# Hashed attention and a channel mix on one core: the last output tile in three column pieces, and a new order of all operations

## The chip, the cores and the metric

The kernel runs on one core of a Trainium2 chip. The metric is device time in microseconds, the median of several runs; a profiled execution gives the trace. The core has five engines with their own instruction streams: TensorE (PE; its weight loads are shown as PEld), VectorE (DVE), ScalarE (ACT), GpSimd (POOL) and SyncE (SP), which here issues nearly all DMA transfers. Every stream is executed in its program order, so an instruction that waits holds up all that stand behind it on its engine or queue.

## What is computed

Two stages, one feeding the other. The first is attention over 4 batches, 8 heads, 768 positions and 64 features, in which a query sees only the keys of its own hash bucket; a bucket is the six signs of a projection. The second mixes each position with the one before it and runs a squared-relu layer with a sigmoid gate.

```python
def _attn_ref(q, k, v, proj):
    ...
    q_bits = (np.einsum('bhsd,dk->bhsk', q, proj) > 0).astype(np.int64)
    k_bits = (np.einsum('bhsd,dk->bhsk', k, proj) > 0).astype(np.int64)
    ...
    mask = q_bucket[:, :, :, None] == k_bucket[:, :, None, :]
    scores = scale * np.matmul(q, k.transpose(0, 1, 3, 2))
    scores = np.where(mask, scores, -1000000000.0)
    ...
    return np.matmul(attn, v).astype(np.float32)

def _moe_ref(x, mu_k, mu_r, w_k, w_v, w_r):
    x_prev = np.concatenate([np.zeros((B, 1, D), dtype=np.float32), x[:, :-1, :]], axis=1)
    xk = mu_k * x + (1.0 - mu_k) * x_prev
    xr = mu_r * x + (1.0 - mu_r) * x_prev
    k = np.maximum(xk @ w_k, 0.0)
    v = k * k @ w_v
    r = 1.0 / (1.0 + np.exp(-(xr @ w_r)))
    return (r * v).astype(np.float32)
```

The attention output, heads side by side, is x: 4 x 768 x 512. The weights are 512 x 1024, 1024 x 512 and 512 x 512.

## The kernel before

**Pairs.** The 32 heads are worked on as 16 pairs n = 0 to 15, four to a batch. For each pair, q, k and v are loaded (ldq, ldv; 384 KB each, pair 0 in quarters of 192 KB). Each side is split into a high and a low fp16 part: hi (lines 535 and 537, for pairs 0 and 1 lines 609 and 611) and lo (line 540, or 614). A transposing DMA (tr, line 544) brings it into the layout for TensorE; pairs 0 and 1 use TensorE transposes instead (line 628), with copies out of PSUM (line 632). The bits matmuls (line 568, or 650 for pair 0) give the sign projections; bx (line 572) turns them into rows, and small DMAs (row, line 592) write these into the same tile as q and k, so that the score matmul adds a penalty for differing buckets by itself. Then follow nine score groups of 1024 columns (sc, line 701), each with its exponential on ScalarE (line 705); the PV matmuls (oo, lines 729 and 734), the first of which reads a column sum of v (the casts and sums va and vsum, lines 482, 490, 493, 496); the normalization (rc and ob, lines 744 to 751); and a transpose of the result into xt, by DMA (otd, line 761) or TensorE (ot, line 787), with small shift copies (xs and xj, lines 769 to 774).

**Channel mix.** VectorE forms the mixed inputs (df, xk and xr, lines 822 to 834). Once four pairs of a batch are ready, its first layer runs in 16 groups (kp, line 852), each evicted by a relu on ScalarE or VectorE (lines 857 and 859) and squared on VectorE (sq, line 862). For each of six row tiles there is a gate matmul (r, line 877), a tanh (line 880), the second layer (v, line 889), the gated product on VectorE (os, line 896) and a store (st, line 900). The weights are loaded in ten pieces of 512 KB (wl, line 428) and cast (wc, lines 431 to 433).

**The order.** Each operation is added to a plan with its engine, what it reads and writes, and an estimated cost. Three tables written into the file then decide everything: `WHERE` gives the engine of operations that may run on several, `SLOT` the PSUM bank of each result, and `ORDER` the place of each operation in one list for all engines. The plan walks that list:

```python
        order = [self.ops[i] for i in ORDER]
        for o in order:
            if o.take is not None:
                name, size = o.take[1], BANKS[o.take[0]]
                self.slot[name] = SLOT[name]
```

So the priorities and costs in the file have no effect on the emitted program; the tables have.

**The last tile.** The last row tile of the last batch is made in two column pieces, in one PSUM bank:

```python
            for lo, hi in ((0, DM // 2), (DM // 2, DM)) if last else ((0, DM),):
                ...
                        r=[...] + ([(nv, 0)] if lo and g == 0 else []),
                        w=[(nv, lo)], take=("sm", nv, 1) if g == 0 and lo == 0 else None, name=nv)
```

The second piece's matmuls come after VectorE's read of the first, since the two share the bank.

Of the kernel before, what the change touches and what calls it, by code (L numbers as in the profile page):

```python
# [32 lines left out]
def X(kind, n):  # L33
    return PX.get(f"{kind}@{n}", 0.0)


def R(kind, n):
# [193 lines left out]
def kernel(  # L231
# [17 lines left out]
    DM = H * D  # L249
# [4 lines left out]
    NFC = DF // P  # L254
# [89 lines left out]
    add = plan.add  # L344
# [613 lines left out]
```

## Time and profile before

| | us |
|---|---|
| median of 3 runs | 250.81 (249.42 to 251.02) |
| profiled execution, its own time | 251.54 |
| its span, first to last instruction | 249.8 |
| TensorE busy | 234.7 (94%) |
| VectorE busy | 196.9 (79%) |
| ScalarE busy | 179.2 (72%) |
| GpSimd busy | 28.6 (11%) |

Times are in microseconds from the span's start unless they are marked otherwise. Matmuls are pipelined, and the mean of one in the profile is longer than the distance from one to the next; the lengths in the chain are such distances. A wait is put down to what ended it. "PEclk" is the TensorE clock that was granted; its mean over the span is 0.998 of full speed. The share of the sixteen DMA engines in a stretch can come out a little over 1, because packets overlap.

### The profile page before, as it was taken

The numbers are of one execution on the slowest core, as the hardware profiler recorded it, in microseconds if no ns is written. First come the engines' busy times: TensorE is split into PE (matmuls) and PEld (weight loads), VectorE is DVE, ScalarE is ACT, GpSimd is POOL, SyncE is SP. The second block draws the span as 40 slices with busy tenths as digits, with TensorE's granted clock in tenths as the row PEclk, the third lists the DMA queues.
The fourth block names the chain that finished last, engine by engine and source line by source line (L and its number), as shares of the span: only waits on it lengthen the run. The fifth ranks groups of instructions, "written<-read, shape, count | busy, mean of one in ns | idle before, by whom it ended". The sixth has DMA issues, their size and how long they took to land.

```text
span 249.8 us, 6514 instructions
## 1 busy us (share of the span) xinstructions
PE 234.7 (94%) x2611; PEld 147.1 (59%) x2611; DVE 196.9 (79%) x471; ACT 179.2 (72%) x224; POOL 28.6 (11%) x75
## 2 busy tenths in 40 slices
PE   7685999999969999999999999999999999999993
PEld 3453778877636656565567576664865654555442
DVE  3997499899879898889998898899697878376322
ACT  4695899999969989896779889988787223332220
POOL 5003141422202410100001100100000000000000
PEclk9999999999999999999999999999999999999999
DMA  6998989999899979899998997792231031022223
GB/s 192 314 199 279 219 269 163 307 175 220 281 332 190 307 152 316 218 187 287 188 342 158 159 186 192 194 235 41 90 64 45 0 129 41 1 84 87 84 85 126
DMA packets 74154, 44.56 MB, mean 178 GB/s; under 512 B 54476, under 2 KB 69132, under 8 KB 74124
## 3 DMA queue, kind: packets, MB, share of 16 engines
q1 hardware_dynamic: 74028, 44.15, 71.6%
q8 instruction: 20, 0.33, 0.5%
q14 instruction: 10, 0.08, 0.1%
q10 hardware_dynamic: 96, 0.01, 0.0%
HBM read 24.12 MB, written 6.29 MB: 122 GB/s over the span
## 4 chain that ended last, share of the span: by engine, by line
PE 81%; DVE 8%; DMA 5%; ACT 1%; SPq 1%; issue 1%; DVEq 0%
PE ps_all L701 21%; PE ps_all L889 17%; PE ps_all L852 16%; PE ps_all L734 13%; PE ps_all L877 8%; PE ps_all L568 4%; DMA nat<-in_q_dram 4%; DMA a<-bx 2%; DVE nh L540 1%; DVE nh L614 1%; PE ps_all L729 1%; DVE a L658 1%; ACT pt L705 1%; SPq L592 1%; PE ps_all L787 1%
## 5 line engine op out<-in xcount | busy, mean ns | idle before, releaser
L705 ACT ACTIVATE pt<-ps_all 128x1024 bf16<-128x1024 f32 x144 | 138.9, 1034 | 21.5 <-PE ps_all L701 20.1
L701 PE MATMUL ps_all<-a 128*128 128x512 f16 (+3 forms) x408 | 79.8, 316 | 3.9 <-DMA a<-bx 2.9
L852 PE MATMUL ps_all<-xk,wk 128*128 128x384 bf16 x256 | 49.0, 326 | 2.3 <-DVE kr L859 2.3
L701 PEld LDWEIGHTS <-a 128*128 128x128 f16 x408 | 35.1, 97 | 25.1 <-DMA a<-bx 3.1
L889 PE MATMUL ps_all<-wv,k 128*128 128x512 bf16 (+1 forms) x200 | 45.9, 370 | 0.6 <-DVE os L896 0.6
L734 PEld LDWEIGHTS <-pt 128*128 128x128 bf16 x1152 | 41.3, 97 | 6.6 <-issue 0.4
L734 PE MATMUL ps_all<-va,pt 128*128 128x65 bf16 x1152 | 43.2, 193 | 0.0
L852 PEld LDWEIGHTS <-wk 128*128 128x128 bf16 x256 | 24.4, 98 | 19.1 <-issue 2.9
L889 PEld LDWEIGHTS <-k 128*128 128x128 bf16 x200 | 19.4, 98 | 20.6 <-issue 0.7
L880 ACT ACTIVATE rs<-ps_all 128x512 f32<-128x512 f32 x24 | 14.2, 601 | 21.0 <-PE ps_all L877 19.1
L857 ACT ACTIVATE kr<-ps_all 128x384 bf16<-128x384 f32 x33 | 15.8, 491 | 17.6 <-DVE k L862 11.2
L896 DVE SCALAR_TENSOR_TENSOR os<-rs,ps_all 128x512 f32<-128x512 f32 (+1 forms) x25 | 16.5, 663 | 14.7 <-PE ps_all L889 9.8
L540 DVE SCALAR_TENSOR_TENSOR nh<-nat,nh 128x768 f16<-128x768 f32 x28 | 26.8, 958 | 1.1 <-ACT nh L535 0.6
L862 DVE TENSOR_TENSOR k<-kr 128x384 bf16<-128x384 bf16 x64 | 22.1, 360 | 3.7 <-ACT kr L857 3.5
L859 DVE TENSOR_SCALAR kr<-ps_all 128x384 bf16<-128x384 f32 x31 | 17.1, 555 | 8.8 <-PE ps_all L852 6.5
L877 PE MATMUL ps_all<-wr,xr 128*128 128x512 bf16 x96 | 23.8, 379 | 0.0
L751 DVE TENSOR_TENSOR ob<-ps_all,rc 128x384 bf16<-128x384 f32 (+1 forms) x36 | 18.3, 511 | 1.0
L877 PEld LDWEIGHTS <-xr 128*128 128x128 bf16 x96 | 9.1, 97 | 9.7
L537 DVE TENSOR_SCALAR nh<-nat 128x768 f16<-128x768 f32 x22 | 12.7, 576 | 1.6 <-DMA nat<-in_q_dram 1.6
L568 PE MATMUL ps_all<-a,p0g 128*32 128x256 f16 (+1 forms) x180 | 13.3, 276 | 0.5 <-DVE ob L751 0.2
L568 PE MATMUL ps_all<-a,p1g 128*32 128x256 f16 (+1 forms) x180 | 12.9, 273 | 0.0
L834 DVE TENSOR_TENSOR xk<-tm,xt 128x768 bf16<-128x768 f16 (+1 forms) x18 | 10.0, 558 | 0.2
(95 smaller groups left out, 187.5 us busy)
## 6 DMA issues: line engine op xcount, KB each, us to landing
vn<-in_v_dram SPq DMA_DIRECT2D x16, 384.0 KB
out_dram<-os SPq DMA_DIRECT2D x23, 256.0 KB
nat<-in_k_dram SPq DMA_DIRECT2D x15, 384.0 KB
nat<-in_q_dram SPq DMA_DIRECT2D x15, 384.0 KB
wst<-in_moe_w_k_dram SPq DMA_DIRECT2D x2, 512.0 KB
wst<-in_moe_w_r_dram SPq DMA_DIRECT2D x2, 512.0 KB
wst<-in_moe_w_v_dram SPq DMA_DIRECT2D x2, 512.0 KB
a<-bx SPq DMA_DIRECT2D x48, 9.0 KB
```

What stands on the lines that cost most here:

```text
L540: nc.vector.scalar_tensor_tensor(out=nh[:, :, D:P], in0=nat.rearrange("p j (c d) -> p (j c) d", d=D), scalar=QS, in1=nh[:, :, 0:D], op0=AL ...
L568: nc.tensor.matmul(ps[g_ * wid : (g_ + 1) * wid, 0:FW], w_[:, m_ - 1 - x : m_ - 1 - x + wid], a_t[sa][:, i, x % NFOLD * FW : (x % NFOLD + ...
L701: nc.tensor.matmul(ps[:, lo - s * w : hi - s * w], side_a["k"][sa][:, j, jc * P : (jc + 1) * P], side_a["q"][sa][:, j, q0 : q0 + hi - lo], ...
L705: nc.scalar.activation(out=pt_t[sp][:, s * w : (s + 1) * w], in_=ps_all[:, plan.slot[nm] * 512 : plan.slot[nm] * 512 + w], func=AF.Exp, bi ...
L734: nc.tensor.matmul(oo[:, (ic - c0) * 65 : (ic - c0) * 65 + 65], pt_t[sp][:, o : o + P], va_t[sa][:, j, jc, 0 : D + 1], start=(not uc and i ...
L751: nc.vector.tensor_tensor(out=ob_t[so][:, c0:c1, j * D : (j + 1) * D], in0=oo[:, :, 0:D], in1=rc_t[sr][:, 1, c0:c1].unsqueeze(2).to_broadc ...
L852: nc.tensor.matmul(ps[:, 0:HALF], wk_sb[:, d, fc * P : (fc + 1) * P], xk_t[mx[d]][:, h * HALF : (h + 1) * HALF], start=(d == 0), stop=(d = ...
L859: nc.vector.tensor_scalar(out=kr_t[sk], in0=sm(nm)[:, 0:HALF], scalar1=0.5 ** 0.5, scalar2=0.0, op0=ALU.mult, op1=ALU.max)
L862: nc.vector.tensor_tensor(out=k2_t[s2][:, h * HALF : (h + 1) * HALF], in0=kr_t[sk], in1=kr_t[sk], op=ALU.mult)
L877: nc.tensor.matmul(sm(nr), xr_t[mx[d]][:, c * P : (c + 1) * P], wr_sb[:, d, :], start=(d == 0), stop=(d == NDC - 1))
L889: nc.tensor.matmul(sm(nv)[:, lo:hi], k2_t[(b * NFC + fc) % NK2][:, c * P : (c + 1) * P], wv_sb[:, fc, lo:hi], start=(fc == 0), stop=(fc == ...
L896: nc.vector.scalar_tensor_tensor(out=os_t[so][:, lo:hi], in0=rs_t[s1][:, lo:hi], scalar=1.0, in1=sm(nv)[:, lo:hi], op0=ALU.add, op1=ALU.mult)
```

## The change

Two things are changed. The last tile is made in three column pieces of 256, 128 and 128, each with a PSUM bank of its own, an own read on VectorE and an own store. And the three tables are replaced as a whole: all operations but those of the last tile stay the same, while their order, the banks and the engine of 88 of them differ. There is no other edit; in the changed file the lines stand one to four further down.

```diff
 WHERE = {
-    "wc0": "DVE", "wc1": "POOL", ... "hi0q0": "ACT", "evt0q00": "DVE", ...
+    "wc0": "POOL", "wc1": "POOL", ... "hi0q0": "DVE", "evt0q00": "ACT", ...
 ...
 ORDER = [
-    0, 2, 3, 4, 5, 6, 7, 8, 1, 67, 64, 98, 99, 25, 9, 35, ...
+    65, 67, 0, 2, 3, 4, 40, 25, 41, 5, 92, 1, 10, 93, 94, 6, ...
 ...
+    LASTCUT = (0, 256, 384, 512)
 ...
-            for lo, hi in ((0, DM // 2), (DM // 2, DM)) if last else ((0, DM),):
+            cut = LASTCUT if last else (0, DM)
+            for lo, hi in zip(cut[:-1], cut[1:]):
+                nv = f"v{b}_{c}" if lo == 0 else f"v{b}_{c}_{lo}"
+                ko = ("os", so) if lo == 0 else ("os2", so, lo)
 ...
-                        r=[...] + ([(nv, 0)] if lo and g == 0 else []),
-                        w=[(nv, lo)], take=("sm", nv, 1) if g == 0 and lo == 0 else None, name=nv)
+                        r=[...],
+                        w=[(nv,)], take=("sm", nv, 1) if g == 0 else None, name=nv)
```

On SP's queue the changed order issues the v loads of pairs 0 and 2 ahead of the k and q loads of pair 3, and the loads of pairs 10 and 11 later than before. In each table the position of an operation can be read off; the prediction counts along them.

More of the change, by code (lines that the diff above doesn't have):

```diff
@@ L891, in add_moe @@
                     add("PE", 4 * MM(hi - lo), T + 0.12 + 0.12 * g, fv,
-                        r=[("wv", fc) for fc in range(4 * g, 4 * g + 4)] + [("k2", (b * NFC + fc) % NK2, h) for fc in range(4 * g, 4 * g + 4) for h in (c // 3,)] + ([(nv, 0)] if lo and g == 0 else []),
-                        w=[(nv, lo)], take=("sm", nv, 1) if g == 0 and lo == 0 else None, name=nv)
+                        r=[("wv", fc) for fc in range(4 * g, 4 * g + 4)] + [("k2", (b * NFC + fc) % NK2, h) for fc in range(4 * g, 4 * g + 4) for h in (c // 3,)],
+                        w=[(nv,)], take=("sm", nv, 1) if g == 0 else None, name=nv)
                 def fo(nv=nv, s1=s1, so=so, lo=lo, hi=hi):
@@ L900, in st @@
                     nc.sync.dma_start(out=rows[:, lo:hi], in_=os_t[so][:, lo:hi])
-                add("DVE", DVE_C(hi - lo), T + PR["os"] + X("os", b), fo, r=[(nv, lo), ("rs", s1)] + ([] if lo == 0 else [("os", so)]), w=[("os", so)] if lo == 0 else [("os2", so)],
-                    give=[nv] if hi == DM else [], name=f"os{b}_{c}")
-                add("SP", 0.45, T + PR["os"] + X("os", b), st, r=[("os", so)] if lo == 0 else [("os2", so)], svc=0.65 if hi - lo == DM else 0.33, off=0.85, land=0.7, name=f"st{b}_{c}")
+                add("DVE", DVE_C(hi - lo), T + PR["os"] + X("os", b), fo, r=[(nv,), ("rs", s1)] + ([] if lo == 0 else [("os", so)]), w=[ko], give=[nv], name=f"os{b}_{c}")
+                add("SP", 0.45, T + PR["os"] + X("os", b), st, r=[ko], svc=0.65 * (hi - lo) / DM + 0.03 * (hi - lo < DM), off=0.85, land=0.7, name=f"st{b}_{c}")
     for n in range(NPAIRS):
```

228 rows, old and new, of tables (ORDER, SLOT, WHERE) are left out of this document.

## The prediction

> **What bounds the kernel now.** I read the page first: busy time, the slices, the DMA rows and the chain.
>
> ```profile
> span 249.8 us, 6514 instructions
> PE 234.7 (94%) x2611; PEld 147.1 (59%) x2611; DVE 196.9 (79%) x471; ACT 179.2 (72%) x224; POOL 28.6 (11%) x75
> ...
> DMA  6998989999899979899998997792231031022223
> ...
> q1 hardware_dynamic: 74028, 44.15, 71.6%
> ...
> HBM read 24.12 MB, written 6.29 MB: 122 GB/s over the span
> ...
> PE 81%; DVE 8%; DMA 5%; ACT 1%; SPq 1%; issue 1%; DVEq 0%
> ```
>
> TensorE is busy for all but 15.1 us, and its work is the same in both kernels, so the change can only move that idle time and the tail. But the DMA engines are full too, from the start until slice 27 (27 x 6.2 = 169 us). Two limits run side by side: TensorE's own work, and the transfers that must have landed before its next work may start. The waits and the stretches (columns after the times: PE, PEld, DVE, ACT, POOL busy, clock, DMA share, GB/s) say where TensorE's idle time lies.
>
> ```profile
> PE ps_all L701 <- DMA a<-bx: 2.9, 1, 2.9
> PE ps_all L852 <- DVE kr L859: 2.3, 1, 2.3
> PE ps_all L628 <- DVE nh L614: 1.4, 2, 1.0
> ...
> PE ps_all L889 <- DVE os L896: 0.6, 1, 0.6
> ...
> 8.00:9.00 1.00, 1.00 (x9) 0.63 (x8) 1.00 (x4) 0.99 (x3) 0.00 (x0) 1.00 1.06 361
> ...
> 20.00:30.00 10.00, 7.09 (x100) 5.05 (x99) 5.10 (x10) 6.98 (x8) 2.90 (x6) 1.00 1.00 253
> ...
> 70.00:80.00 10.00, 7.38 (x76) 4.72 (x74) 8.34 (x16) 7.82 (x11) 1.43 (x3) 1.00 1.07 260
> ...
> 170.00:180.00 10.00, 10.00 (x158) 6.74 (x157) 7.91 (x24) 7.68 (x9) 0.00 (x0) 1.00 0.17 60
> 240.00:250.00 10.00, 5.98 (x35) 3.22 (x33) 2.43 (x5) 1.58 (x3) 0.00 (x0) 0.93 0.28 106
> ```
>
> The idle time sits ahead of 30 us, at 70 us and in the tail; from 80 to 240 us TensorE hardly stops. The clock is full. The chain (start, length, what) shows that both large holes are late transfers:
>
> ```profile
> 20.91 4.03 DMA a<-bx
> ...
> 65.69 5.27 DMA nat<-in_q_dram
> ...
> 143.91 0.84 PE ps_all L568 x24
> ```
>
> At 20.91 a small sign-row transfer takes 4.03 us because it queues behind loads. At 65.69 pair 8's q load takes 5.27 us; VectorE stands at hi8 until it lands, and the PSUM evictions behind hi8 are what line 852 waits for (2.3).
>
> **The price of a transfer.** One 384 KB load (393 kB) at 361 GB/s and a share of 1.06 is 1.15 us of all sixteen engines; 512 KB of weights is 1.54, an output tile 0.77, a quarter-pair load 0.58, sign rows nearly nothing. The queue's total is 71.6% of 249.8 = 178.9 us. HBM traffic, 30.41 MB at that rate, is 89.3; the rest, 89.6 us, belongs to 28 transposes of twelve blocks and 11 of six, 33.5 whole ones: an estimate of 2.67 us each (1.33 for a small one).
>
> **The queue test.** For each point where TensorE waits for a transfer I add up the transfers up to and including it on SP's queue, and TensorE's own work ahead of it in program order. The work is counted in the order at the paces of the chain:
>
> ```profile
> 103.25 1.73 PE ps_all L889 x8
> ...
> 115.66 0.87 PE ps_all L701 x5
> ...
> 153.85 0.65 PE ps_all L852 x4
> ...
> 159.49 1.09 PE ps_all L734 x36
> ```
>
> That is 0.216 us for 512 columns, two score groups in 0.87, 0.163 for 384 columns, 0.030 for 65. Transfer sum minus work is the idle time that the order forces, less a lag that is alike for both orders. Check on before: the last transpose of pair 7 has four quarter loads, 20 loads, two weights and twelve transposes up to it, 2.3 + 23.0 + 3.1 + 32.0 = 60.4 us; TensorE reached that pair's bit matmuls (line 568) at 63.66, as the timeline has it (start, length, what, idle time before and what ended it; hi8's row stands below it):
>
> ```profile
> 63.66 0.69 PE L568 MATMUL ps_all<-a,p0g 128*32 128x256 f16 x4 [0.21 <-DVE ob L751]
> ...
> 70.99 0.56 DVE L537 TENSOR_SCALAR nh<-nat 128x768 f16<-128x768 f32 x1 [1.56 <-DMA nat<-in_q_dram]
> ```
>
> So the lag is at most 3.3 us, and 60.4 + 3.3 leaves no slack. Work ahead of it is 50.0, so 10.4 us are forced beside the lag.
>
> **Part one, the order.** In the changed order the same matmuls stand behind 55 score groups instead of 51; 53.0 us of work covers 62.0 us of transfers (one weight more): 9.0 are forced. Pairs 10 to 14 give 11.8, 11.1, 11.6, 12.7, 10.8 before and 8.9, 9.3, 8.0, 9.6, 9.3 after. Idle time once taken stays, so the largest counts: 12.7 before, 9.6 after, a relief of 3.1 us. Pair by pair from 7 to 15 the mean relief is 1.9. Before reached pair 13's bits at 143.91 where its floor is 137.9 + 3.3 = 141.2, so it lost 2.7 more to other things. If the new order loses the same above its own floor, the relief is what comes out. I take 2.5, between 1.9 and 3.1. Ends: nothing (the time comes back as waits on other engines), and 3.1 + 2.7 if those go too.
>
> The opening gives nothing by this test: ahead of pair 1's second row transfer both orders have four quarter loads, ten loads and two transposes, 19.2 us, under the same 14.7 us of work. New there: two v loads are issued earlier and keep the queue fed, so the 4.03 us wait may shrink by up to its 2.9 of idle; but pair 2's rows, now with 22.6 us of transfers under 18.6 of work where it was 21.5 under 20.1, take it back. I put zero, with 0 and 2.9 us of gain as the ends.
>
> At hi8 the new order puts two evictions of line 859 ahead of the waiting hi8 on VectorE. Queued behind it are then lo8 and the later evictions, and meanwhile TensorE has three score groups, the rest of a PV group and two first-layer groups (about 2.8 us) of work that needs none of them. That covers a wait like the 1.56 us of this trace; without the cover the 2.3 us stall returns. What is late next are the loads of pairs 10, 11 and 14, which stand some 10 us deeper in the queue (94.2, 108.5 and 136.8 us of transfers): VectorE or ScalarE would stand there. At 3.3 to 6.3 us of lag (hi8 had the upper one: it began at 70.99 with 64.7 us of transfers) they force idle time only up to 17.1, at pairs 10 and 14, which before had passed by then as well.
>
> **Part two, other engines.** In net numbers eleven first steps of the v sums, six second steps, one third step, two v casts, three weight casts (one of them off VectorE) and two small copies go to GpSimd.
>
> ```profile
> L490 DVE TENSOR_TENSOR vt<-va 128x390 f32<-128x390 bf16 x7 | 3.9, 558 | 0.0
> ...
> L493 DVE TENSOR_TENSOR vt<-vt 128x130 f32<-128x130 f32 x4 | 1.2, 295 | 0.6 <-POOL vt L490 0.5
> ...
> L482 POOL CAST va<-vn 128x768 bf16<-128x768 f32 x6 | 6.0, 1001 | 24.2 <-DMA vn<-in_v_dram 16.9 <-PE ps_all L734 5.3 <-PE ps_all L701 2.0
> L496 POOL TENSOR_TENSOR vsu<-vt 128x130 bf16<-128x130 f32 x5 | 2.4, 477 | 18.5 <-DVE vt L493 16.8 <-PE ps_all L568 1.7
> L493 POOL TENSOR_TENSOR vt<-vt 128x130 f32<-128x130 f32 x4 | 1.7, 436 | 12.0 <-DVE vt L490 12.0
> L431 POOL CAST wk<-wst 128x1024 bf16<-128x1024 f32 x1 | 1.0, 1040 | 0.0
> L490 POOL TENSOR_TENSOR vt<-va 128x390 f32<-128x390 bf16 x1 | 0.8, 837 | 0.0
> ```
>
> VectorE is relieved of 11 x 0.56 + 7 x 0.29 and about 1.8 for casts, 10.0 us; GpSimd gains 11 x 0.84 + 7 x 0.44 + 2 x 1.00 + 3 x 1.04 and about 1 for copies, 18.5 us on 28.6. Its idle time (89%) hides that, so I put it at zero. Without cover it is the third rival. Switched hi, relu and copy operations between ScalarE and VectorE nearly cancel in count: zero.
>
> GpSimd's work could also slow VectorE. The trace has one sign of it, the third figure here (shortest, median, longest, ns):
>
> ```profile
> L537 DVE TENSOR_SCALAR nh<-nat x22: 547/552/1062, 9.6 to 148.4; 128x768 f16<-128x768 f32 x22
> ```
>
> One of 22 took 0.51 us longer than the median. The Trainium skill, "SBUF — State Buffer" (section "SBUF: two separate sides"), says that the two engines share a port pair as an exclusive lock, held for a whole instruction, so that the later one stands still. By that rule at its worst, every added GpSimd microsecond is taken from VectorE; this trace's one long case in 22 is far from that.
>
> **Part three, the last tile.** Now two pieces of 256 columns share one bank, so the second waits for VectorE's read of the first:
>
> ```profile
> 243.04 1.90 PE L889 MATMUL ps_all<-wv,k 128*128 128x512 bf16 x12
> ...
> 245.04 0.42 DVE L896 SCALAR_TENSOR_TENSOR os<-rs,ps_all 128x256 f32<-128x256 f32 x1 [0.24 <-PE ps_all L889]
> 245.51 1.03 PE L889 MATMUL ps_all<-wv,k 128*128 128x256 bf16 x8 [0.57 <-DVE os L896]
> ...
> 246.58 0.42 DVE L896 SCALAR_TENSOR_TENSOR os<-rs,ps_all 128x256 f32<-128x256 f32 x1 [1.12 <-PE ps_all L889]
> ```
>
> ```profile
> L896 DVE SCALAR_TENSOR_TENSOR os<-rs,ps_all 128x512 f32<-128x512 f32 x23 | 15.6, 684 | 13.4 <-PE ps_all L889 8.5 <-ACT rs L880 2.8 <-ACT kr L857 1.1
> ...
> L900 SPq DMA_DIRECT2D out_dram<-os x25: 332/333/819, 114.2 to 247.0; - x25
> ```
>
> The tile begins four 512-column matmuls after 243.04, at 243.90. After: eight matmuls of 256 and sixteen of 128 columns at the same pace per column, 1.75 us, with nothing between; 0.20 from there to VectorE (246.58 less 245.51 less 0.87); a 128-column read, by the slope from 0.68 at 512 columns to 0.42 at 256, 0.29. It ends at 246.14 instead of 247.00: 0.86 us gained.
>
> The extra store issue, 0.33, fits in the 0.44 us between the second and third read; uncovered it would leave 0.53. Eight more matmuls and weight loads are in the pace.
>
> **Sum.** 2.5 + 0.86 = 3.36. The profiled execution took 251.54 us around its span of 249.8, which becomes 248.2; it was 0.73 above the median, so on the median of 250.81 the forecast is 247.5 us.
>
> **Rivals.** First, the order gives back what it gains: TensorE was 94% busy, and VectorE, ScalarE and the queue are all near full before 80 us, so a stall taken from one shows at the next. Then only the tail counts: 250.0. This is also how it comes out if the reorder doesn't do what it says.
>
> Second, all that before lost above its floor goes as well: 250.81 - 0.86 - 3.1 - 2.7 = 244.1. For it speaks that hi8 alone was 2.3; against it, that other waits of this sort were all over the opening.
>
> Third, slower: the v sums on GpSimd. Each tile's PV begins with a matmul that reads the sum, and everything behind it on TensorE waits. A whole chain is 0.84 + 0.44 + 0.48 on GpSimd against 0.56 + 0.29 + 0.29, 0.6 us more, and in order: pair 4's last step now stands behind pair 5's cast, which waits for pair 5's load (52.0 us of transfers). Eleven of these are 6.6 us; with half uncovered, 250.81 - 0.86 + 3.3 = 253.3. A harsher form is VectorE standing still while GpSimd works (the 0.51 us above): at its worst the added 18.5 less the relief of 10.0 is lost, 247.5 + 8.5 = 256.0; I give it 0.03 of the case's 0.20. The chain decides from about 0.3 us of uncovered wait per moved chain on. Against it: the order leaves most of the sums of pairs 7 to 14 several microseconds ahead of their matmul.
>
> **How the numbers follow.** Forecast 0.47, tail only 0.23, all gone 0.10, slower 0.20. A measurement of this kernel tells about 1% from no change (249.42 to 251.02 here), so faster means below 248.3. The forecast's own spread (245 to 249) gives 0.40 faster and 0.07 within; tail only 0.20 within and 0.03 slower; all gone 0.10 faster; the slower case 0.17 slower and 0.03 within. Together 0.50, 0.30, 0.20. The range runs from near the second rival to near the third, 244.5 to 253.0.
>
> **What would show it.** Right: pair 7's bits start near 62.0 + 3.3 = 65.3 with four score groups more behind them; pair 13's by 141.5; no wait of line 852 above 1 us around 70 us; the last tile's matmuls without a stop. Wrong: waits of the PV matmuls for GpSimd sums; VectorE or ScalarE standing at the loads of pairs 10, 11 or 14 with evictions behind; pair 13's bits later than 144.

## The result: slower by 1.0 to 1.5%, and the profile after

The changed kernel took 253.68 us (252.56 to 253.93, four runs) beside 250.92 for the kernel before: ratio 1.015, interval 1.0108 to 1.0192; a second series gave 1.0139 (1.0080 to 1.0197). Ratios, here and below, are of fast runs alone, since some executions fall into a slower state; the medians of all runs give 1.011 and 1.010. The forecast was 247.5. The profiled execution, at 252.56 us the quickest of its four, stands only 1.0 us over the profiled one of before, so the two traces show less than half of the 2.8 us between the medians; more traces follow below. The page:

```profile
span 250.8 us, 6530 instructions
...
PE 236.3 (94%) x2619; PEld 147.8 (59%) x2619; DVE 191.2 (76%) x449; ACT 178.2 (71%) x223; POOL 50.0 (20%) x99
...
PE 74%; DMA 9%; DVE 9%; SPq 4%; issue 2%; ACT 1%; DVEq 0%
```

GpSimd has 21.4 us more (18.5 were worked out), but VectorE only 5.7 less, where 10.0 were worked out. In the chain TensorE fell from 81% to 74%. The stretches of before (first fence) and after (second; PE, PEld, DVE, ACT, POOL busy, clock, DMA share, GB/s):

```profile
18.00:26.00 8.00, 5.09 (x61) 3.48 (x58) 6.05 (x11) 4.59 (x6) 2.14 (x5) 1.00 0.91 274
60.00:90.00 30.00, 27.05 (x343) 17.95 (x342) 25.88 (x62) 26.69 (x34) 6.02 (x10) 1.00 0.97 249
```

```profile
18.00:26.00 8.00, 6.30 (x65) 3.98 (x66) 6.16 (x11) 6.35 (x8) 0.00 (x0) 1.00 0.64 138
60.00:90.00 30.00, 27.22 (x347) 17.93 (x348) 28.65 (x62) 25.61 (x30) 12.64 (x18) 1.00 0.95 250
```

Two things stand out: from 18 to 26 us the transfer queue is a third empty, and from 60 to 90 us VectorE is busy 28.65 of 30 us, beside a GpSimd with twice the work. What TensorE waits for (total, times, longest):

```profile
PE ps_all L702 <- DMA a<-bx: 2.5, 4, 1.0
PE ps_all L702 <- ACT pt L706: 1.8, 4, 0.8
PE ps_all L629 <- DVE nh L615: 1.7, 2, 1.2
...
PE ps_all L853 <- DVE kr L860: 1.1, 2, 0.9
```

No wait for GpSimd is among them. The two large holes of before (2.9 and 2.3) are gone, and many of about half a microsecond took their place. The chain from 66 to 84 us shows why:

```profile
66.91 3.38 DMA a<-bx
70.28 0.54 DVE ob L752
...
73.15 1.01 DVE kr L860 x2
...
74.46 0.95 DVE tm L831
...
76.36 0.77 DVE nh L538
77.13 0.90 DVE k L863
...
80.28 0.78 DVE nh L538
81.09 0.96 DVE nh L541
...
83.38 0.34 PE ps_all L730
```

For 13 us the chain hardly leaves VectorE. And several of its instructions are stretched. The timeline of VectorE and GpSimd in the changed kernel:

```profile
74.46 0.83 POOL L483 CAST va<-vn 128x768 bf16<-128x768 f32 x1 [6.88 <-DMA vn<-in_v_dram]
74.46 0.94 DVE L831 TENSOR_SCALAR tm<-df,mu 128x384 f16<-128x384 bf16 x1
...
75.36 0.85 POOL L491 TENSOR_TENSOR vt<-va 128x390 f32<-128x390 bf16 x1
75.43 1.00 DVE L835 TENSOR_TENSOR xk<-tm,xt 128x384 bf16<-128x384 f16 x1
...
76.66 1.16 POOL L483 CAST va<-vn 128x768 bf16<-128x768 f32 x1
...
77.05 0.97 DVE L863 TENSOR_TENSOR k<-kr 128x384 bf16<-128x384 bf16 x1
...
78.93 0.81 PE L853 MATMUL ps_all<-xk,wk 128*128 128x384 bf16 x4 [0.94 <-DVE kr L860]
```

An operation of 0.35 us (line 863) takes 0.97 when it falls on a GpSimd cast, and ends 0.21 us after that. In the two traces of the changed kernel all four executions of this line that took over 0.3 us too long ended 0.21 to 0.22 us after the GpSimd instruction they met, however long they were. The relu eviction behind it (line 860) is what TensorE then waits for. Executions of three lines, by the tiles they work on (shortest, median, longest, ns):

```profile
L831 DVE TENSOR_SCALAR tm<-df,mu x20: 276/416/1187, 38.3 to 133.2; 128x768 f16<-128x768 bf16 x12, 128x384 f16<-128x384 bf16 x8
L863 DVE TENSOR_TENSOR k<-kr x64: 310/351/973, 77.0 to 241.1; 128x384 bf16<-128x384 bf16 x64
L860 DVE TENSOR_SCALAR kr<-ps_all x29: 508/550/558, 73.1 to 233.2; 128x384 bf16<-128x384 f32 x29
```

Line 860 reads PSUM and is never stretched. I call *excess* the time of VectorE's instructions above the median of their line and shape, where that is over 0.06 us. Before it is 3.5 us in 9 instructions, after 9.8 us in 26, and each of the 35 overlaps a GpSimd instruction, although in the changed kernel only 101 of VectorE's 449 instructions meet one; 4.7 of the 9.8 lie between 60 and 80 us. The Trainium skill, "SBUF — State Buffer" (section "SBUF: two separate sides"), which the prediction cited, describes such a lock, held for a whole instruction; this trace agrees with it.

For all traces I also took TensorE's *lost time*: the start of an instruction less TensorE's work ahead of it, by the prediction's paces. In us, with a second trace where there is one (the kernel with the new tail alone is the first experiment, the lighter kernels come later):

| lost up to | before | new tail alone | changed | changed, lighter | new tail, lighter |
|---|---|---|---|---|---|
| 30 us | 12.0 | 13.5, 10.7 | 12.0, 11.8 | 11.6 | 10.4 |
| 50 us | 13.9 | 15.4, 13.2 | 15.0, 15.0 | 14.8 | 13.0 |
| 60 us | 14.7 | 16.3, 13.6 | 16.2, 16.0 | 16.2 | 13.3 |
| 90 us | 18.7 | 18.4, 17.1 | 20.5, 20.9 | 17.3 | 15.6 |
| end | 21.4 | 20.7, 19.4 | 22.4, 23.2 | 20.2 | 17.6 |

What the changed kernel loses more, it loses ahead of 90 us; behind that point the kernels lose much alike. Up to 30 us the traces do not tell old and new apart (10.4 to 13.5 against 11.6 to 12.0).

### The profile page after: what moved, and what is told of

It reads as the page before. It is cut to its first block, busy times and chain, and to the rows that moved or that the text cites. A ratio compares the mean times of both kernels' runs of the same rounds, so it can differ in the third digit from the quotient of the medians.

```text
span 250.8 us, 6530 instructions
## 1 busy us (share of the span) xinstructions
PE 236.3 (94%) x2619; PEld 147.8 (59%) x2619; DVE 191.2 (76%) x449; ACT 178.2 (71%) x223; POOL 50.0 (20%) x99
## 4 chain that ended last, share of the span: by engine, by line
PE 74%; DMA 9%; DVE 9%; SPq 4%; issue 2%; ACT 1%; DVEq 0%
PE ps_all L702 18%; PE ps_all L893 17%; PE ps_all L853 14%; PE ps_all L735 10%; PE ps_all L878 8%; DMA a<-nh 4%; PE ps_all L569 4%; DMA a<-bx 2%; DMA nat<-in_k_dram 2%; SPq L545 2%; DVE nh L541 1%; DVE nh L538 1%; DVE kr L860 1%; DVE a L659 1%; ACT pt L706 1%
## 5 line engine op out<-in xcount | busy, mean ns | idle before, releaser
L706 ACT ACTIVATE pt<-ps_all 128x1024 bf16<-128x1024 f32 x144 | 139.1, 1035 | 20.5 <-PE ps_all L702 19.5
L702 PE MATMUL ps_all<-a 128*128 128x256 f16 (+3 forms) x408 | 81.3, 316 | 5.0 <-DMA a<-bx 2.5
L735 PEld LDWEIGHTS <-pt 128*128 128x128 bf16 x1152 | 43.0, 97 | 6.1 <-issue 0.2
L893 PE MATMUL ps_all<-wv,k 128*128 128x512 bf16 (+2 forms) x208 | 46.5, 363 | 0.0
L735 PE MATMUL ps_all<-va,pt 128*128 128x65 bf16 x1152 | 45.0, 193 | 0.0
L858 ACT ACTIVATE kr<-ps_all 128x384 bf16<-128x384 f32 x35 | 16.8, 490 | 23.5 <-PE ps_all L853 14.5
L863 DVE TENSOR_TENSOR k<-kr 128x384 bf16<-128x384 bf16 x64 | 22.4, 375 | 6.0 <-ACT kr L858 5.8
L900 DVE SCALAR_TENSOR_TENSOR os<-rs,ps_all 128x512 f32<-128x512 f32 (+2 forms) x26 | 16.5, 642 | 11.8 <-PE ps_all L893 8.7
L881 ACT ACTIVATE rs<-ps_all 128x512 f32<-128x512 f32 x24 | 14.4, 602 | 15.5 <-PE ps_all L878 10.3
L860 DVE TENSOR_SCALAR kr<-ps_all 128x384 bf16<-128x384 f32 x29 | 15.8, 550 | 5.2 <-PE ps_all L853 4.5
L538 DVE TENSOR_SCALAR nh<-nat 128x768 f16<-128x768 f32 x24 | 14.8, 618 | 3.8 <-DMA nat<-in_q_dram 3.7
L483 POOL CAST va<-vn 128x768 bf16<-128x768 f32 x8 | 7.7, 956 | 37.3 <-DMA vn<-in_v_dram 28.1
L569 PE MATMUL ps_all<-a,p0g 128*32 128x256 f16 (+1 forms) x180 | 13.2, 276 | 0.8 <-DMA a<-nh 0.6
L573 DVE TENSOR_SCALAR bx<-ps_all 128x256 uint16<-128x256 uint16 x15 | 6.3, 422 | 8.9 <-PE ps_all L569 8.7
```

Source lines behind the costliest of these rows:

```text
L538: e.tensor_scalar(out=o, in0=x, scalar1=QS, scalar2=None, op0=ALU.mult)
L569: nc.tensor.matmul(ps[g_ * wid : (g_ + 1) * wid, 0:FW], w_[:, m_ - 1 - x : m_ - 1 - x + wid], a_t[sa][:, i, x % NFOLD * FW : (x % NFOLD + ...
L702: nc.tensor.matmul(ps[:, lo - s * w : hi - s * w], side_a["k"][sa][:, j, jc * P : (jc + 1) * P], side_a["q"][sa][:, j, q0 : q0 + hi - lo], ...
L706: nc.scalar.activation(out=pt_t[sp][:, s * w : (s + 1) * w], in_=ps_all[:, plan.slot[nm] * 512 : plan.slot[nm] * 512 + w], func=AF.Exp, bi ...
L735: nc.tensor.matmul(oo[:, (ic - c0) * 65 : (ic - c0) * 65 + 65], pt_t[sp][:, o : o + P], va_t[sa][:, j, jc, 0 : D + 1], start=(not uc and i ...
L860: nc.vector.tensor_scalar(out=kr_t[sk], in0=sm(nm)[:, 0:HALF], scalar1=0.5 ** 0.5, scalar2=0.0, op0=ALU.mult, op1=ALU.max)
```

## The experiments

Ratios are to the kernel before, run beside them, with the 95% interval. "Old" and "new" are the tables of before and of the change; every kernel here has the three-piece last tile.

**The tail alone, and the engines apart.** Theory A: GpSimd's added work holds VectorE up. Theory B: the order itself is at fault, by late sign rows and transposes.

```diff
 # tail3: ORDER, SLOT, WHERE old, except the last tile
-1379, 1378, 1380, 1381, 1382, 1383, 1384, 1385, 1386,
+1379, 1378, 1380, 1383, 1381, 1382, 1384, 1385, 1387, 1388, 1386, 1389, 1390,
 # poolback: ORDER, SLOT new;  poolmoved: ORDER, SLOT old
 # moved = the 42 operations on GpSimd in exactly one of the two tables
+WHERE.update({k: OLD_WHERE[k] for k in moved})     # poolback
+WHERE.update({k: NEW_WHERE[k] for k in moved})     # poolmoved
```

> The kernel before with its own order, banks and engines, and only the last tile cut into the three pieces with banks of their own. The prediction's part three says 0.86 us less than before: ratio 0.9966, about 249.9 us beside 250.8. Theory 'the order or the engines lose the time': as just said, and the last tile's matmuls without a stop. Theory 'the tail loses it' (more, smaller matmuls and one store more): at or above before, 250.8 to 253.

> The kernel before with the three-piece tail alone, once more: 0.9966 of before by the 0.86 us of the prediction's part three, 0.9969 measured the first time.

> The changed kernel, with its order and banks, but the 42 operations that moved to or from GpSimd back on the engine they had before. Theory A (GpSimd's added work holds VectorE up: the changed trace has 9.8 us of VectorE time above the medians of its forms, all of it under a GpSimd instruction, before 3.5): the excess falls to some 3.5 us and the time to 249.5 to 251. Theory B (the order itself lost it, the engines are innocent): 252.5 to 256, since VectorE, full from 60 to 80 us, gets some 6 us of net work back.

> The kernel before with its own order and the three-piece last tile, and the same 42 operations on the engines that the change gives them. Theory A (GpSimd's work holds VectorE up): 1.5 to 4 us slower than the kernel with the three-piece tail alone, so 251.5 to 254, with 8 us or more of VectorE excess under GpSimd instructions. Theory B (the order lost it): within 1 us of the kernel with the three-piece tail alone, 249 to 251.

> The changed kernel once more, for a second trace of it and its time beside these: its profiled run was at 252.56 us with a span of 250.8, the lowest of four with median 253.68. Both theories: 253.0 to 254.0. Theory A expects VectorE's excess under GpSimd near 10 us again; theory B expects the same waits for sign rows (a<-bx) at about 30 us and 60 to 70 us.

Measured: the tail alone 0.9969 (0.9925 to 1.0013) and again 0.9929 (0.9890 to 0.9968); about 0.995 together, a version slightly ahead of both kernels. The changed kernel again 1.0139, with an excess of 10.3 us. The operations moved in the old order: 1.0111 (1.0051 to 1.0170), excess 8.0 us, the time and excess that theory A had forecast. But this does not show the cause: from 60 to 90 us its excess was 2.4 us only, and TensorE waited 3.3 us for late v sums, at 26.7 and 40.0 us, which is another price of the moved work:

```profile
PE ps_all L730 <- POOL vsu L497: 1.7, 1, 1.7
PE ps_all L730 <- DVE vsu L497: 1.6, 1, 1.6
```

The operations put back in the new order: 1.0292 (1.0226 to 1.0357), 257.4 us, although its excess was only 3.4. Theory A as I had put it, that taking the work off GpSimd heals the new order, fell; theory B's figure was passed on the other side. TensorE's waits in that kernel:

```profile
PE ps_all L730 <- POOL vsu L497: 2.3, 1, 2.3
PE ps_all L629 <- DVE nh L615: 2.2, 3, 1.3
PE ps_all L730 <- POOL xt L384: 2.0, 1, 2.0
```

The first wait, at 85.5 us, is for a v sum that ends late because its first steps stand in VectorE's queue behind other work (the third names an operation long done, so what ended that wait is not known). This suggests, without showing it, that in this order VectorE has no room for the work, on its own stream or beside GpSimd; this kernel's granted clock was also 0.94 from 60 to 90 us. To see what the work costs it must be left out.

**Less of the work, and more of it.** One kernel leaves part of GpSimd's work out; the same cut in the old order is the control; one leaves out the weight casts alone; one adds idle work on GpSimd. In the kernels with fewer weight casts VectorE also clears the weights once, at the start.

```diff
 # lite: tables new;  liteold: tables old, also for casts on VectorE
+few = i in (0, 1, 2)
-nc.gpsimd.tensor_copy(dst, stage)
+nc.gpsimd.tensor_copy(dst[:, :, 0:16] if few else dst, ...)
+few = n in (5, 6, 7)
-copy(va_t[sa][:, :, :, 0:D], vn)
+copy(va_t[sa][:, :, :, 0:W0], vn[:, :, :, 0:W0])       # W0 = 8 if few, as in the first v sum
 # litewc: the first cut alone
 # dummy: tables old
+for n, s in ((5, 7), (5, 2), (5, 6), (5, 0), (6, 5), (6, 6), (6, 7), (6, 8), (7, 3), (7, 6), (6, 1)):
+    nc.gpsimd.tensor_tensor(out=junk, in0=pt[:, lo:lo+390], in1=pt[:, lo+390:lo+780], op=ALU.add)
```

> The changed kernel with some GpSimd work between 55 and 86 us left out: of the first three weight casts only 16 of 512 columns are cast (the weights are cleared by VectorE at the start), of the v casts and first v-sum steps of pairs 5 to 7 only 8 columns each. Order, banks and engines are the change's; some 8 us of GpSimd's time go. Theory A (GpSimd's instructions hold VectorE up, and VectorE is the bound from 60 to 88 us): VectorE's excess from 60 to 80 us falls from 4.7 us to under 1.5, and the time by 1.5 to 2.5 us, to 251.0 to 252.2. Theory B (the order's rows and transposes come late, VectorE's excess would have been waited for anyway): within 0.5 us of the changed kernel, 253.1 to 254.1.

> The kernel before with the three-piece tail, with the same work left out as in the changed kernel's lighter form (16 of 512 columns of three weight casts, 8 columns of the v casts and first v-sum steps of pairs 5 to 7), whichever engine does it here. Theory A (the changed order pays for GpSimd's instructions at VectorE): this order has only 3 to 4 us of that work on GpSimd and 1.5 us of VectorE excess behind it, so it gains less, at most 1 us: ratio 0.993 to 0.998. Rival (leaving that work out is worth 3 us in any order): 2.5 us or more below the three-piece tail alone, a ratio under 0.987.

> The changed kernel with the three early weight casts on GpSimd cut to 16 of 512 columns (the weights cleared by VectorE at the start), and the v casts and sums whole. Theory A by the excess: these casts stand over 1.8 of the 4.7 us of VectorE's excess from 60 to 80 us, so a third to a half of the lighter form's 3 us comes back: 252.0 to 252.8. Rival (the casts are late for the first-layer matmuls and that is the whole cost): all 3 us, 250.5 to 251.3. Theory B: no change, 253.1 to 254.1.

> The kernel before with the three-piece tail, and eleven more GpSimd additions of 128x390 (0.84 us each, 9.2 us in all) between 58 and 84 us, whose results nobody reads: each follows the exponential of one score group. Theory A: VectorE's excess grows by 3 to 5 us and the time by 1 to 2.5 us over the kernel with the three-piece tail alone: 250.2 to 251.7. Theory B: within 0.5 us of that kernel, 248.7 to 249.7.

Measured: the lighter changed kernel 1.002 (0.9987 to 1.0054), 1.2% or 3 us under the changed one; more than the 1.5 to 2.5 expected. The lighter old one 0.9942 (0.9905 to 0.9978), hardly below the new tail alone, so the cut is worth 3 us in the new order and less than 1 in the old. The stretch from 60 to 90 us, first of the lighter changed kernel, then of the lighter old one:

```profile
60.00:90.00 30.00, 29.62 (x365) 19.66 (x366) 27.43 (x68) 28.17 (x32) 6.92 (x16) 1.00 1.01 261
```

```profile
60.00:90.00 30.00, 28.58 (x345) 18.60 (x342) 24.21 (x63) 27.58 (x34) 4.25 (x12) 1.00 1.03 265
```

With 5.7 us less on GpSimd, VectorE gets through more instructions (68 for 62) in less busy time, its excess between 60 and 80 us falls from 4.7 to 1.3 us, and TensorE loses 1.1 us there instead of 4.3. That is theory A, in its second form: the new order spends VectorE to the last from 60 to 90 us, and GpSimd's added work then costs about 3 us through it. In the changed kernel TensorE never waited for a result of GpSimd, and VectorE only once, for 0.3 us; so what the cut removes is the stretching and not the waiting for results: the excess from 60 to 90 us fell by 2.9 us, TensorE's loss by 3.2. About half a microsecond of VectorE's own work (the first v sum of pair 7) went with the cut.

The weight casts alone gave 1.012 (1.0074 to 1.0167), some 0.6 us, below the 0.8 to 1.6 expected, although the excess from 60 to 80 us fell from 4.7 to 2.2. So excess is not a price by itself. The chain above shows why: they run at 63.7 to 67.3 us, where the sign rows (3.38 us, landing at 70.28) end last anyway; the v casts and sums run from 74.5 us on, where VectorE ends last.

The added work on the old order cost far more than expected, 1.0196 (1.0136 to 1.0256), but not only by the lock. Its waits and stretches:

```profile
PE ps_all L570 <- DVE ob L753: 2.5, 1, 2.5
PE ps_all L854 <- POOL wk L433: 2.0, 1, 2.0
```

```profile
60.00:70.00 10.00, 7.04 (x93) 4.42 (x89) 5.33 (x14) 6.73 (x8) 5.23 (x10) 0.83 0.89 230
70.00:80.00 10.00, 8.10 (x50) 4.62 (x51) 8.06 (x15) 5.64 (x8) 3.65 (x5) 0.83 0.85 227
```

A weight cast stood behind the idle additions in GpSimd's stream, and the granted clock averaged 0.83 over these 20 us. As a price of the lock this run is spoiled.

**Where in time.** One order up to a point, the other from there; banks were given anew where two results met.

```diff
+first, then = old, new        # oldthennew: K = 670; oldshort: K = 350; old30: K = 156
+first, then = new, old        # new30: K = 155
+ORDER = first[:K] + [i for i in then if i not in first[:K]]
+WHERE = first's for operations in first[:K], then's for the others
```

> The order and engines of the kernel before up to 86.6 us of TensorE work (about 105 us), and from there the changed order and engines, with the three-piece tail. In the traces the changed kernel loses 2 us more than the kernel before up to 90 us and the same amount behind it. If that is so: 248.5 to 250, as the three-piece tail alone. If GpSimd's added work costs everywhere: above 251.

> The order and engines of the kernel before up to 42.5 us of TensorE work (about 56 us), then the changed ones, with the three-piece tail. If the loss lies between 56 and 90 us (both theories A and B place it there): 252.3 to 254. If it lies in the first 56 us and the rest only carries it: 249 to 250.5.

> The order and engines of the kernel before up to 18.5 us of TensorE work (about 30 us), then the changed ones, with the three-piece tail. If the opening's loss is made in the first 30 us (theory Q): as the run that goes over at 56 us, 1.003 to 1.009 of before. If it is made between 30 and 56 us: as the changed kernel, 1.012 to 1.018.

> The changed order and engines up to 18.1 us of TensorE work (about 30 us), then those of the kernel before, with the three-piece tail. Theory Q: 1.3 to 2 us above the three-piece tail alone, 1.002 to 1.006 of before. If the first 30 us cost nothing: 0.995 to 0.999.

Measured, beside 0.995 for all old and 1.0145 for all new:

| old up to | ratio | interval |
|---|---|---|
| 105 us | 0.9988 | 0.9955 to 1.0022 |
| 56 us | 1.0064 | 1.0027 to 1.0100 |
| 30 us | 1.0081 | 1.0051 to 1.0112 |
| new to 30 us, then old | 1.0050 | 1.0013 to 1.0088 |

The new order costs 0.6 to 1.0% (1.6 to 2.5 us) in its first 30 us, 0.2% from 30 to 56 (within the error), 0.8% (1.9 us) from 56 to 105, and 0.4% (1.0 us) behind it, where the intervals overlap. The intervals reach 0.3 to 0.6% to each side, so all these sizes are rough. My reading that both theories' place, 56 to 90 us, held it all was half of the truth: the opening is the other half.

**The opening.** Sign rows ahead of loads, loads into the empty stretch, and GpSimd out of the way:

```diff
 # row2first: new order, loads 222 (pair 4 q) and 295 (pair 5 k) behind pair 2's rows
-..., 233, 222, 108, ..., 154, 295, 184, 183, 241, ...
+..., 233, 108, ..., 154, 184, 183, 222, 295, 241, ...
 # row1first: old order, loads 222 and 223 (pair 4 q, k) behind pair 1's rows (129 the second)
-..., 135, 222, 229, 230, 223, 34, ..., 40, 129, 139, ...
+..., 135, 229, 230, 34, ..., 40, 129, 222, 223, 139, ...
 # feed: new order, 222 and 71 (pair 1 v) behind pair 2's first transpose (180)
-..., 127, 180, 77, ..., 200, 71, 107, 305, 233, 222, 108, ...
+..., 127, 180, 222, 71, 77, ..., 200, 107, 305, 233, 108, ...
 # v0later: new order, 68 (pair 0 v) behind 180
-..., 178, 68, 104, ..., 127, 180, 77, ...
+..., 178, 104, ..., 127, 180, 68, 77, ...
```

> The changed kernel with two loads (pair 4's q, pair 5's k; 2.3 us of transfers) issued behind pair 2's sign rows instead of ahead of them. Every trace of the changed order shows a wait of 1.2 to 1.7 us for those rows near 29 us, which the order before does not have. Theory O (the opening's loss of some 2 us is this wait): the wait goes and the time falls by 1.0 to 1.7 us, to 251.9 to 252.7. Rival (the queue is the bound in the opening, what is taken from one transfer is given to the next): the wait goes, the transposes of pairs 3 to 6 come as late as before, within 0.5 us of 253.6.

> The kernel before with the three-piece tail, and two loads (pair 4's q and k) issued behind pair 1's sign rows instead of ahead of them. Its traces show TensorE waiting 1.4 to 3.2 us for those rows at 22 us. Theory O (the opening's waits for sign rows count): 1 to 2 us below the three-piece tail alone, a ratio of 0.989 to 0.993. Rival (the queue is the bound, the loads are late next): within 0.5 us of it, 0.995 to 0.999.

> The changed kernel with two loads (pair 4's q, pair 1's v; 2.3 us of transfers) issued between the two transposes of pair 2, at about 16.5 us, instead of at 22.7 and 23.2 us. Theory Q (the opening's loss is the queue running dry from 18 to 26 us): the share in these 8 us rises from about 0.65 to 0.85 or more and the time falls by 1 to 2 us, to 251.6 to 252.6. Rival (pair 2's second transpose and pair 1's rows then land later, and TensorE waits for them): the dry stretch goes, the waits at 23 to 25 us grow by 1 to 2 us, time within 0.5 us of 253.6 or above.

> The changed kernel with pair 0's v load issued behind pair 2's first transpose, at about 16.5 us, instead of at 4.3 us. GpSimd's cast and sums of pair 0 then run behind 20 us, where VectorE's work for pairs 1 and 2 is done, and the dry stretch of the queue gets 1.15 us of transfers. Theory G (GpSimd over VectorE counts in the opening as it does from 60 to 90 us): VectorE's excess of 1.05 us from 10 to 20 us goes, pair 2's second transpose is issued about 1 us earlier (17.2 instead of 18.2 us), and the time falls by 1 to 2 us, to 251.6 to 252.6. Rival (the transposes are late by VectorE's order of work, not by its pace): the excess goes, the time stays within 0.5 us of 253.6.

Measured: rows of pair 2 first 1.0203 (1.0158 to 1.0247), rows of pair 1 first 1.0112 (1.0054 to 1.0170). Both are slower than their partners, by 1.5 and 4 us: theory O fell, and even its rival was too kind. Later loads make the next thing late, as the second kernel's waits and its stretch from 20 to 24 us show; the queue's share there is 0.35, and the wait for a transpose (a<-nh) comes in addition.

```profile
PE ps_all L702 <- DMA a<-bx: 1.8, 2, 1.2
PE ps_all L569 <- DMA a<-nh: 1.3, 1, 1.3
```

```profile
20.00:24.00 4.00, 2.79 (x33) 1.93 (x32) 1.78 (x3) 2.85 (x3) 0.96 (x3) 1.00 0.35 110
```

Feeding the empty stretch of the new order: 1.0113 (1.0057 to 1.0169), at most 0.8 us gained of the 1 to 2 expected. The stretch is full, and a wait that the changed kernel did not have there comes instead:

```profile
18.00:26.00 8.00, 5.43 (x61) 3.51 (x57) 5.88 (x11) 6.07 (x7) 3.13 (x5) 1.00 1.08 238
```

```profile
PE ps_all L569 <- DMA a<-nh: 1.3, 1, 1.3
```

So the empty queue is a sign, not the cause: pair 2's transposes come late, and what is issued early lands ahead of them. Their issues on SP's queue in the changed kernel (first) and with the new tail alone:

```profile
L545 SPq DMA_TRANSPOSE a<-nh x2: 1537/1810/2084, 14.9 to 18.2; - x2
```

```profile
L545 SPq DMA_TRANSPOSE a<-nh x2: 1557/1802/2048, 11.6 to 15.0; - x2
```

In the changed kernel both are some 3.2 us later: in the new order VectorE comes to pair 2's q side last, behind pair 1's and several evictions. With pair 0's v load issued later, GpSimd does nothing from 10 to 20 us instead of 3.63, and VectorE's excess of 1.05 us there is gone:

```profile
10.00:20.00 10.00, 8.60 (x82) 5.03 (x81) 9.61 (x19) 9.09 (x14) 0.00 (x0) 1.00 0.95 248
```

It ran at 1.0078 (1.0046 to 1.0111), 0.7% or 1.7 us under the changed kernel, as theory G forecast. But in its trace, of a run of 254.56 us where the median was 252.41, the second transpose was issued at 17.87 us, 0.3 us earlier and not 1, so the mechanism is not shown. The edit also moves the load itself behind the transpose in the queue. Pair 0's early v load, or the GpSimd work that it starts, is likely part of the opening's loss; how much of it is the lock stays open, as does the share of VectorE's own order.

## Why the prediction was wrong, by its own steps

**Part one** took its 2.5 us from "if the new order loses the same above its own floor". This step failed. The floors of the queue test had no meaning where TensorE was later than they: pair 7's bits came at 69.3 us instead of 65.3, pair 13's at 145.7 instead of 141.5.

```profile
L569 PE MATMUL ps_all<-a,p0g x12: 272/273/283, 69.3 to 69.8; 128*32 128x256 f16 x12
...
L569 PE MATMUL ps_all<-a,p0g x4: 283/284/284, 145.7 to 145.7; 128*32 128x256 f16 x4
```

The floor of pair 13 by the test was 135.6 of transfers less 126.0 of work, 9.6, and 3.3 of lag; the kernel had lost some 7 more on the way. A floor says what an order can't beat, and I read it as what it would reach. The relief is not quite nothing: freed of part of GpSimd's work, the new order loses 1.1 us from 60 to 90 us, the old one with the same cut 2.3.

**The opening** was put at zero with ends of 0 and 2.9 us of gain, without an end for a loss. It cost 1.6 to 2.5 us. I had counted transfers and TensorE's work there, but not when VectorE would have the transposes' input ready; the numbers that spoke against the change (pair 2's rows, 22.6 of transfers under 18.6 of work) I let cancel.

**Part two** put GpSimd's work at zero because GpSimd was idle 89% of the time. This step failed too, with the largest price, about 3 us by the lighter kernel. GpSimd's idle time hides its own work, not what it does to VectorE. The harsher form of the third rival, at 0.03, was the mechanism from 60 to 90 us; its worst case of 18.5 us did not come, the excess grew by 6.3 us. I had sized it by one line, 537, with one long case of 22; over all of VectorE's lines before had nine, 3.5 us for 28.6 us of GpSimd. The slope was there to read: with the 18.5 us forecast for GpSimd it gives 2.3 us, with the measured 21.4 it gives 2.6, still under half of the 6.3 that came, and the lines of the channel mix (830 to 862), which work on 16-bit data, make up most of it. The chain form of that rival was wrong for this kernel: no PV matmul waited for a v sum. That its 253.3 lies near the measured time is luck.

**Part three** was right. The last tile's matmuls run on without a stop (32 with the tile before it):

```profile
243.93 3.66 PE L893 MATMUL ps_all<-wv,k 128*128 128x512 bf16 x32
...
247.62 0.29 DVE L900 SCALAR_TENSOR_TENSOR os<-rs,ps_all 128x128 f32<-128x128 f32 x1 [0.16 <-PE ps_all L893]
```

Eight of them belong to the tile before, so the last begins 8 x 0.216 after 243.93, at 245.66, and its last read ends at 247.91: 2.25 us, where 2.24 was worked out and before took 3.10. The kernel with the tail alone gained 0.3 and 0.7%, 0.8 to 1.8 us, for the 0.86. The loads of pairs 10, 11 and 14, which I expected late next, were not waited for: rightly put at nothing.

The sum with the measured terms: 0.9 to 1.2 gained in the tail; some 2 lost in the opening, 0.4 from 30 to 56 us, 1.9 from 56 to 105 us (about what the 3 of GpSimd's work less the 1.2 of relief would leave) and 1.0 behind it. That is about 4 us lost on balance, against 3.6 by the ratios and 2.8 between the medians.

## What to carry to other kernels

An idle engine is a free place for work only if its work does not hold up the engine that ends last: before moving work from VectorE to GpSimd, sum VectorE's excess over all its lines and scale it by the GpSimd time to be added. Here this gives 2.6 us where 6.3 came, so take it as the least to expect, and look stretch by stretch where VectorE ends last, since only there it costs time. A queue floor that falls by 3 us is a gain only where the kernel stands on that floor; first look at how far above it the old kernel ran, and which engine fills the room. When two orders are compared, run each up to a point and the other from there: four such kernels placed the loss in the first 30 us and between 56 and 105 us, which the traces alone, with 1 us between them, did not.

## What the runs showed of the hardware that I had not expected

VectorE instructions that read PSUM were not slowed by GpSimd: in the nineteen traces of this case VectorE has 328 instructions of over 0.06 us excess, each of which overlaps a GpSimd instruction, and none of them reads PSUM. The relu evictions of 128x384 met a GpSimd instruction 104 times and took at most 559 ns, their usual time. Instructions on data in SBUF were slowed: the squares of 128x384 (16-bit) took 588 ns on the mean of 109 meetings, 350 otherwise.

The 0.83 of TensorE's granted clock in the kernel with idle GpSimd work is half speed for 3.4 us in each stretch of 10 us, from 65.1 and from 71.9 us. Each spell began about half a microsecond after a stop ended (2.5 us until 64.61, 2.0 us until 71.49). In the trace of before the clock stayed at 1.00 through stops of 2.9 and 2.3 us, so the length of a stop alone does not decide it.

Executions of the same tables differ mostly in the opening: in seven traces with the old first 50 us, TensorE had lost 12.9 to 15.4 us at that point; four traces of the changed opening had 14.8 to 15.7. The one with 15.4, of the new tail alone, had run at half clock for 3.4 us from 25.0 us.
